# Weights turned into float32 in pieces of 768 columns, under a planner that books the SBUF port of GpSimd and VectorE

## The chip, the core and the metric

One core of a Trainium2 chip. The time is that of the device for one run of the program, in microseconds (us), here the median of three runs. Engines, as the profile names them: PE is TensorE's matmuls, PEld its weight loads, DVE is VectorE, ACT ScalarE, POOL GpSimd, SP the queue that issues the DMAs.

## The reference, cut to what matters

```python
def _attn_ref(x, weight_gen):               # x: 2 x 4096 x 192, weight_gen: 2 x 4096 x 8 x 7
    w = softmax(weight_gen, axis=-1)
    # token s: sum over the 7 taps of w[s, head, tap] * x[s - 6 + tap, head's 24 columns]
    out = np.einsum('bshk,bskhg->bshg', w, x_unf)

def _moe_ref(x, w_in, w_out):               # 8192 x 192, 192 x 2048, 2048 x 192
    h = x @ w_in
    g = h * np.cos(h)
    return g @ w_out

def _moe2_ref(x, w_in, w_out):
    h = x @ w_in
    g = np.maximum(0.01 * h, h)
    return g @ w_out

return _moe2_ref(_moe_ref(_attn_ref(x, weight_gen)))
```

The four weight matrices arrive as float64.

## The kernel before

**Tiling.** The 8192 tokens are cut into 16 blocks of 512. For each block the attention is a sum of seven products on VectorE (lines 385 to 414, tiles `pr` and `xa`; for blocks 0 and 1 the sum is made by PE, lines 461 to 476), which PE turns over so that columns lie on partitions. Then come the two layers, `m` = 0 and 1. A layer of one block is 16 chunks of 128 hidden columns. A chunk is ten matmuls of 512 columns: five make `h` (line 645, function `hidden`), five add its share to the block's output (`project_hi`, lines 694 to 696, and `project_lo`, lines 699 and 700). Every operand of a matmul is split in a rounded part `hi` and a remainder `lo`, which is why there are five.

**Between the two halves of a chunk.** In layer 0: ACT makes `g` from `h` (`turns`, line 657), DVE takes whole turns off (`angle`, 664), ACT takes the sine (669), DVE multiplies by `h` (`times`, 672), ACT rounds to `hi` (line 230, a helper), POOL subtracts to `lo` (line 235, a helper). In layer 1: ACT twice (681 and 230), then DVE for `lo`. `h` lies in PSUM, in one of three banks that chunks may hold; `g`, `hi` and `lo` lie in SBUF. So `angle` and `times` read PSUM, while the attention's `pr` and `xa` read and write SBUF alone.

**Weights.** A layer's weights come in four groups (four chunks each), so there are eight groups, and all eight are needed early, since a first block of layer 1 starts at chunk 32 of 512. A group comes in four pieces: `a` (128 x 512), `r` (128 x 256) of the first matrix, and `0` and `2` (128 x 384 each) of the second. Each piece is loaded as float64 words and then goes through ACT (`size`, line 564), POOL (`clamp`, 567), DVE (`shift`, 572), DVE (`merge`, 578), ACT (`low`, 585), POOL (`add`, 590); then `hi` parts are rounded (line 230 or 232) and POOL subtracts the `lo` parts (line 235: tiles `ilo`, `wlo`, `olo`, `or`).

**What sets the order.** `Plan` holds every operation with a due time, a cost for each engine that may do it, and its dependencies. `emit` walks through a plan's time and writes each engine's instructions down in that order. On the chip each engine then takes its own list strictly in order and waits by semaphores; nothing of the plan's times is left there. A cost that is written as a tuple is that of a DVE operation on SBUF alone; before, such a cost is multiplied by `SHARED` = 1.55 while POOL is busy.

Of the kernel before, what the change touches and what calls it, by code (L numbers as in the profile page):

```python
# [11 lines left out]
I32 = mybir.dt.int32  # L12
# [26 lines left out]
class Op:  # L39
    def __init__(self, due, cost, fn, deps, bufs):  # L40
        self.due, self.cost, self.fn, self.bufs = due, cost, fn, bufs
        self.deps, self.next, self.ready, self.end = len(deps), [], 0.0, None
        for d in deps:
            d.next.append(self)


class Plan:


    HOP = 0.08  # L50
    SLACK = 0.5
    NEAR = 0.12
# [3 lines left out]
    SHARED = 1.55  # L56
# [27 lines left out]
    def emit(self):  # L84
        free = dict.fromkeys(("PE", "ACT", "DVE", "POOL", "SP"), 0.0)
        wire = 0.0
# [5 lines left out]
        def start_of(o, e):  # L92
            t = max(o.ready + (self.SLACK if e == "PE" else 0.0), free[e], wire - 2.0 if e == "SP" else 0.0)
            if e == "SP" and o.due > self.at + self.AHEAD:
                return None
            for b in o.bufs:
# [8 lines left out]
            return t  # L105

        left = len(self.ops)
        while left:
            best = None
            for e in free:  # L110
# [10 lines left out]
                if at:  # L121
                    t0 = min(a[0] for a in at)
                    t, _, o = min((a for a in at if a[0] <= t0 + self.NEAR), key=lambda a: a[1])
                    if best is None or t < best[0]:
                        best = t, e, o
# [3 lines left out]
            if isinstance(cost, tuple):  # L129
                cost = cost[0] * (self.SHARED if free["POOL"] > t else 1.0)  # L130
# [25 lines left out]
            for n in o.next:  # L156
                n.ready = max(n.ready, o.end + self.HOP)
# [10 lines left out]
def conv_attention_moe_moe(ctx, tc, x, weight_gen, w_in1, w_out1, w_in2, w_out2, out):  # L168
# [27 lines left out]
    SUMMED = {0, 1}  # L196
    PACE = {0: 0.4, 1: 0.6}
# [81 lines left out]
    def softmax(s0, s1, due):  # L279
# [20 lines left out]
        op(due - 5, {"DVE": 0.2 + 0.95 * part}, lambda e: nc.vector.tensor_reduce(  # L300
            out=M(), in_=W(), axis=AX.X, op=ALU.max), [k], [k], bufs)
        op(due - 4, {"DVE": (0.2 + 0.85 * part,), "POOL": 0.3 + 1.6 * part}, lambda e: wide(e, ALU.subtract), [k], [k], bufs)
        op(due - 3, {"ACT": 0.2 + 0.8 * part + (2.6 if s0 else 0)}, lambda e: nc.scalar.activation(
            out=W(), in_=W(), func=AF.Exp), [k], [k], bufs)
        op(due - 2, {"DVE": 0.2 + 0.95 * part}, lambda e: nc.vector.tensor_reduce(
            out=M(), in_=W(), axis=AX.X, op=ALU.add), [k], [k], bufs)
        op(due - 2, {"DVE": 0.25}, lambda e: nc.vector.tensor_scalar(
            out=M(), in0=M(), scalar1=1e-9, scalar2=None, op0=ALU.add), [k], [k], bufs)
        op(due - 1, {"DVE": 0.25 + 0.7 * part}, lambda e: nc.vector.reciprocal(out=M(), in_=M()), [k], [k], bufs)
        op(due - 1, {"DVE": (0.2 + 0.85 * part,)}, lambda e: wide(e, ALU.mult), [k], [k], bufs)  # L310
# [40 lines left out]
    def attention(b, begins):  # L351
# [10 lines left out]
        for q0, q1, e0 in parts:  # L362
# [11 lines left out]
            for i, k in enumerate(reversed(range(K))):  # L374
# [4 lines left out]
                cost = (0.09 + 0.195 * n,) if e0 == "DVE" else 0.3 + 0.6 * n  # L379
# [42 lines left out]
                if e0 == "DVE":  # L422
                    main, rest = (cost[0] * 0.75,), (0.36 if n == Q else 1.1,)
# [19 lines left out]
    def attention_summed(b, begins):  # L443
# [7 lines left out]
        for i, k in enumerate(reversed(range(K))):  # L451
# [27 lines left out]
            op(due, {"DVE": (0.87,)}, product, reads, [("pr", b, k)], [xt, smw, pr])  # L479
            op(due + 0.5, {"PE": 0.9}, total, [("pr", b, k), "ident"] + ([("tm", b)] if i else []), [("tm", b)], [pr, tm])  # L480
            if i:
# [5 lines left out]
                op(due + 0.4, {"DVE": (0.36,)}, total_rest, keys, [("xbr", b, 0)], bufs)  # L487
# [17 lines left out]
    def place(m, b, due, key, src, v):  # L505
# [15 lines left out]
    def weights(m, g):  # L521
# [9 lines left out]
        def load(i, raw):  # L531
            if i == "a":
                nc.sync.dma_start(out=raw().rearrange("p c w -> p (c w)"), in_=wi[:P, c2])
            else:
                c = slice((g * GF + i) * P, (g * GF + i + 2) * P)
                nc.sync.dma_start(
                    out=raw().rearrange("p f d w -> p f (d w)"), in_=wo[c, :].rearrange("(f p) d -> p f d", p=P)
                )

        def load_rest(raw, j):  # L540
            c = slice(c2.start + 2 * j * half, c2.start + 2 * (j + 1) * half)
            nc.sync.dma_start(out=raw()[j * R : (j + 1) * R].rearrange("p c w -> p (c w)"), in_=wi[P:, c])

        for i in ("a", "r", 0, 2):
            shape = {"a": [GF * P], "r": [half]}.get(i, [2, D])
            w = math.prod(shape) / 512
            due = need[m, g * GF + (i or 0 if i in (0, 2) else 0)] + {"a": -0.6, "r": -3.0}.get(i, 1.8)
            raw = temp([P] + shape + [2], "raw", RAW, f"w{n}{i}", I32)
            t = temp([P] + shape, "wa", WA, f"wt{n}{i}", I32)
            v = temp([P] + shape, "wn", WN, f"wn{n}{i}", I32)  # L550
            k = n, i
            if i == "r":
                for j in range(2):
                    op(due - 6, {"SP": 0.4}, lambda e, raw=raw, j=j: load_rest(raw, j), (), [("raw", k, j)], [raw])
                kr = [("raw", k, 0), ("raw", k, 1)]
            else:
                op(due - 6, {"SP": 3.2 * w}, lambda e, i=i, raw=raw: load(i, raw), (), [("raw", k)], [raw])
                kr = [("raw", k)]

            def high(raw=raw):  # L560
                return raw()[..., 1]

            def size(e, t=t, high=high):
                nc.scalar.activation(out=t().bitcast(F32), in_=high().bitcast(F32), func=AF.Abs)

            def clamp(e, t=t):
                eng[e].tensor_scalar(
                    out=t().bitcast(F32), in0=t().bitcast(F32), scalar1=MOST, scalar2=LEAST, op0=ALU.min, op1=ALU.max
                )

            def shift(e, t=t):
                nc.vector.tensor_scalar(
# [229 lines left out]
```

## Time and profile before

| | us |
|---|---|
| three runs | 1287.0, 1287.84, 1288.92 |
| median | 1287.84 |
| the profiled execution | 1289.18 |
| its span, first to last instruction | 1287.2 |
| PE busy | 1233.0 (96%) |
| DVE busy | 933.4 (73%) |
| ACT busy | 883.4 (69%) |
| POOL busy | 489.0 (38%) |

The busy time of PE is made up of 5120 matmuls of 512 columns, the same number in any version of this kernel, and some transposes and sums with 128 columns. What can be gained or lost is time in which PE waits or runs at the lower clock, and that lies where other engines deliver too late. So the profile is read by stages of the span.

### The profile page before, as it was taken

How to read it: one execution, taken by the hardware profiler on the slowest of the kernel's cores; microseconds unless marked ns; L12 is line 12 of the kernel's file. 1: busy time of each engine (PE TensorE's matmuls, PEld its weight loads, DVE VectorE, ACT ScalarE, POOL GpSimd, SP SyncE). 2: the span in 40 equal slices, each digit the busy share in tenths (PEclk: the TensorE clock that was granted, in tenths of full speed). 3: DMA queues.
4: the chain of work that ended last, by engine and by line, in shares of the span. 5: the costliest groups of instructions: out<-in, count | busy, mean ns of one | idle time of the engine just before them, and what ended most of it. 6: DMA issues, size and time to landing. Idle time of an engine off the chain costs nothing.

```text
span 1287.2 us, 15419 instructions
## 1 busy us (share of the span) xinstructions
PE 1233.0 (96%) x5416; PEld 995.6 (77%) x5416; DVE 933.4 (73%) x1343; ACT 883.4 (69%) x1642; POOL 489.0 (38%) x398
## 2 busy tenths in 40 slices
PE   5798799999999999999999999999999999999998
PEld 4576587777778878787788878788787877888886
DVE  7998998889875776849795595866869586554333
ACT  4688776787776766767676666667676676776654
POOL 5898872566332322323323232322323232232000
PEclk8999899999999999999999999999999999999999
DMA  5231420100001000010100101010010100000000
GB/s 162 79 127 52 143 72 13 58 32 1 1 1 44 1 15 29 1 58 1 43 1 2 43 1 44 1 51 1 1 44 1 44 1 13 1 1 13 1 13 25
DMA packets 15037, 39.50 MB, mean 31 GB/s; under 512 B 1781, under 2 KB 8307, under 8 KB 14961
## 3 DMA queue, kind: packets, MB, share of 16 engines
q1 hardware_dynamic: 14960, 38.53, 9.1%
q8 instruction: 42, 0.69, 0.2%
q14 instruction: 35, 0.28, 0.1%
HBM read 30.13 MB, written 6.29 MB: 28 GB/s over the span
## 4 chain that ended last, share of the span: by engine, by line
PE 58%; DVE 28%; ACT 7%; issue 4%; POOL 1%; DMA 1%; SPq 0%; ACTq 0%; DVEq 0%; POOLq 0%
PE h L645 29%; DVE pr L392 5%; DVE g L672 4%; DVE g L664 4%; PE acc1r L696 3%; PE acc1m L700 3%; PE acc1m L694 3%; PE acc1m L695 3%; PE acc1r L699 3%; PE acc0m L694 3%; DVE xa L399 3%; PE acc0r L696 3%; PE acc0m L695 3%; DVE lo L235 3%; PE acc0r L699 2%
## 5 line engine op out<-in xcount | busy, mean ns | idle before, releaser
L235 POOL TENSOR_TENSOR lo<-g,hi 128x512 fp32r<-128x512 f32 x256 | 358.6, 1402 | 622.1 <-ACT hi L230 552.9
L235 DVE TENSOR_TENSOR lo<-h,hi 128x512 fp32r<-128x512 f32 x256 | 175.5, 687 | 167.5 <-ACT hi L230 165.0
L669 ACT ACTIVATE g<-g 128x512 f32<-128x512 f32 x256 | 161.5, 631 | 146.5 <-DVE g L664 145.9
L672 DVE TENSOR_TENSOR g<-h,g 128x512 f32<-128x512 f32 x256 | 175.1, 687 | 82.9 <-ACT g L669 81.5
L664 DVE SCALAR_TENSOR_TENSOR g<-g,h 128x512 f32<-128x512 int32 x256 | 173.8, 681 | 56.6 <-ACT g L657 55.0
L681 ACT ACTIVATE h<-h 128x512 f32<-128x512 f32 x256 | 149.0, 582 | 86.2 <-PE h L645 85.6
L657 ACT ACTIVATE g<-h 128x512 int32<-128x512 f32 x256 | 151.2, 591 | 61.0 <-PE h L645 60.0
L230 ACT ACTIVATE hi<-g 128x512 fp32r<-128x512 f32 x242 | 152.0, 630 | 36.2 <-DVE g L672 34.2
L230 ACT ACTIVATE hi<-h 128x512 fp32r<-128x512 f32 x256 | 151.4, 592 | 6.5 <-PE acc1r L696 0.2
L694 PE MATMUL acc0m<-hi,ohi 128*128 128x512 f32 x256 | 105.0, 410 | 16.5 <-ACT hi L230 14.9
L645 PE MATMUL h<-x0hi,ihi 128*128 128x512 f32 x256 | 102.4, 400 | 4.1 <-DVE g L672 2.7
L699 PE MATMUL acc0r<-lo,or 128*128 128x512 f32 x256 | 102.4, 400 | 3.0 <-POOL lo L235 3.0
L699 PE MATMUL acc1r<-lo,or 128*128 128x512 f32 x256 | 100.6, 393 | 3.7 <-DVE lo L235 3.6
L694 PE MATMUL acc1m<-hi,ohi 128*128 128x512 f32 x256 | 102.5, 400 | 0.1
L645 PE MATMUL h<-x1hi,ihi 128*128 128x512 f32 x256 | 101.8, 398 | 0.8 <-DVE g L672 0.8
L645 PE MATMUL h<-x0rh,r 128*128 128x512 f32 x256 | 101.0, 395 | 1.1 <-ACT x0rh L230 1.1
L695 PE MATMUL acc1m<-hi,olo 128*128 128x512 f32 x256 | 100.1, 391 | 1.8 <-POOL olo L235 1.8
L645 PE MATMUL h<-x1hi,ilo 128*128 128x512 f32 x256 | 100.5, 393 | 1.4 <-POOL ilo L235 1.4
L645 PE MATMUL h<-x0lo,ihi 128*128 128x512 f32 x256 | 100.6, 393 | 0.7 <-DVE x0lo L235 0.7
L645 PE MATMUL h<-x0hi,ilo 128*128 128x512 f32 x256 | 100.8, 394 | 0.0
L645 PE MATMUL h<-x0rl,r 128*128 128x512 f32 x256 | 100.6, 393 | 0.0
L645 PE MATMUL h<-x1rl,r 128*128 128x512 f32 x256 | 100.3, 392 | 0.1
(227 smaller groups left out, 2529.4 us busy)
## 6 DMA issues: line engine op xcount, KB each, us to landing
xt<-in_x SPq DMA_DIRECT2D x14, 960.0 KB, 4.8
w<-in_moe_w_out SPq DMA_DIRECT2D x16, 384.0 KB, 3.2
out<-osb SPq DMA_DIRECT2D x16, 384.0 KB, 2.6
smw<-in_weight_gen SPq DMA_DIRECT2D x3, 448.0 KB, 5.5
r<-whi SPq DMA_DIRECT2D x16, 64.0 KB, 3.1
r<-wlo SPq DMA_DIRECT2D x16, 64.0 KB, 2.1
xt<-in_x SPq DMA_DIRECT2D x1, 768.0 KB, 10.2
xt<-in_x SPq DMA_DIRECT2D x2, 283.5 KB
```

The costliest lines, as they stand in the source:

```text
L230: nc.scalar.activation(out=out, in_=in_, func=AF.Copy)
L235: eng[e].tensor_tensor(out=out, in0=a, in1=b.bitcast(F32), op=ALU.subtract)
L645: nc.tensor.matmul(h(), w[:, c], v(), start=i == 0, stop=i == len(terms) - 1)
L657: nc.scalar.activation(out=k, in_=h(), func=AF.Copy, scale=0.5 / math.pi, bias=0.25)
L664: nc.vector.scalar_tensor_tensor(out=g(), in0=g().bitcast(I32), scalar=-2 * math.pi, in1=h(), op0=ALU.mult, op1=ALU.add)
L669: nc.scalar.activation(out=g(), in_=g(), func=AF.Sin, bias=math.pi / 2)
L672: nc.vector.tensor_tensor(out=g(), in0=h(), in1=g(), op=ALU.mult)
L681: op(pos + 0.6, {"ACT": 0.58}, lambda e: nc.scalar.activation(out=h(), in_=h(), func=AF.Prelu, alpha=0.01), [kh], [kg], [h])
L694: nc.tensor.matmul(am(), ohi[:, f % GF, :], ghi(), start=first, stop=False)
L695: nc.tensor.matmul(am(), olo[:, f % GF, :], ghi(), start=False, stop=False)
L696: nc.tensor.matmul(ar(), orr[:, f % GF, :], ghi(), start=first, stop=False)
L699: nc.tensor.matmul(ar(), orr[:, f % GF, :], glo(), start=False, stop=last)
```

## The change

The notes at the planner's constants, and the operations, change in three ways.

**The pieces.** A group of weights now comes in two pieces, `in` (the old `a` and `r` side by side) and `out` (the old `0` and `2`), 128 x 768 each. The loads stay as they were, but `size`, `clamp`, `shift`, `merge`, `low` and `add` run over 768 columns at once; only for the first group, `PARTED`, are they kept apart (512 and 256, 384 and 384). The roundings and remainders of `out` also run over all four chunks of a group at once. The tiles `raw`, `wa` and `wn` have two buffers each instead of three.

**The early chunks.** For odd chunk numbers below `EARLY` = 34 in layer 0, `times` writes back into the PSUM bank of `h`, `hi` is rounded from there, and `lo` is made by DVE instead of POOL. There are 16 such chunks. Their bank is held until `lo` is made.

**The planner.** A variable `port` is set to the end of every POOL operation and of every DVE operation with a tuple as its cost, and such an operation is not planned to start before it; the factor 1.55 goes. Many costs are written anew, the time from PE to another engine gets `DRAIN` = 0.17 on top, and among operations that could start within `NEAR` = 0.6 the earliest due time wins, with a penalty for idle time. `turns`, `hi` of layer 1, `size` and `low` may now also go to DVE.

The core of the diff:

```diff
-    HOP = 0.08
+    HOP = 0.06
     SLACK = 0.5
-    NEAR = 0.12
+    NEAR = 0.6
+    IDLE = 20.0
 ...
-    SHARED = 1.55
+    DRAIN = 0.17
+    YIELD = 0.01
 ...
+            if e == "POOL" or isinstance(o.cost[e], tuple):
+                t = max(t, port)
 ...
             if isinstance(cost, tuple):
-                cost = cost[0] * (self.SHARED if free["POOL"] > t else 1.0)
+                cost = cost[0]
+                port = t + cost
+            elif e == "POOL":
+                port = t + cost
 ...
-        for i in ("a", "r", 0, 2):
-            shape = {"a": [GF * P], "r": [half]}.get(i, [2, D])
+        U = 3 * half
+        for i in ("in", "out"):
 ...
+            if (m, g) not in PARTED:
+                parts, loaded = [(0, U)], [loaded[0] + loaded[1]]
 ...
-            op(pos + 0.5, {"ACT": 0.58}, turns, [kh], [kg], [h, g])
+            op(pos + 0.5, {"ACT": 0.58, "DVE": 0.67}, turns, [kh], [kg], [h, g])
 ...
-            op(pos + 2.0, {"POOL": 1.42}, lambda e: minus(e, glo(), g(), ghi()), [kg, khi], [klo], [g, ghi, glo])
+            if bank_low:
+                op(pos + 1.4, {"DVE": 0.67}, times, [kg], [kh], [h, g])
+                op(pos + 1.7, {"ACT": 0.585, "DVE": 0.67}, lambda e: copy(e, ghi(), h()), [kh], [khi], [h, ghi])
+                op(pos + 2.0, {"DVE": 0.67}, lambda e: minus(e, glo(), h(), ghi()), [kh, khi], [klo], [h, ghi, glo])
 ...
-            op(pos + 1.0, {"ACT": 0.58}, lambda e: copy(e, ghi(), h()), [kg], [khi], [h, ghi])
+            op(pos + 1.0, {"ACT": 0.58, "DVE": 0.67}, lambda e: copy(e, ghi(), h()), [kg], [khi], [h, ghi])
```

What it moves, by the order of the built programs. PE's 5198 rows are the same work in another order. First POOL, the list around the remainders of the second group (`01`), before:

```order
L567 TENSOR_SCALAR wt01r_304<-wt01r_304 128x256
L567 TENSOR_SCALAR wt01a_298<-wt01a_298 128x512
L590 TENSOR_TENSOR wn01r_316<-wt01r_304,wn01r_316 128x256
L235 TENSOR_TENSOR wlo01_344<-wn01r_316,whi01_338 128x256
L590 TENSOR_TENSOR wn01a_313<-wt01a_298,wn01a_313 128x512
L567 TENSOR_SCALAR wt010_352<-wt010_352 128x384
L235 TENSOR_TENSOR lo_0_376<-g_0_289,hi_0_362 128x512
L235 TENSOR_TENSOR ilo01_85<-wn01a_313,ihi01_84 128x512
L235 TENSOR_TENSOR olo00_82<-wn002_278,ohi00_81 128x256
L235 TENSOR_TENSOR or00_83<-wn002_278,or00_83 128x2x64
L235 TENSOR_TENSOR lo_1_410<-g_1_327,hi_1_399 128x512
```

and POOL at the same place now:

```order
L607 TENSOR_SCALAR wt01in_278<-wt01in_278 128x768
L264 TENSOR_TENSOR olo00_82<-wn00out_208,ohi00_81 128x256 x2
L264 TENSOR_TENSOR or00_83<-wn00out_208,or00_83 128x2x64 x2
L631 TENSOR_TENSOR wn01in_287<-wt01in_278,wn01in_287 128x768
L264 TENSOR_TENSOR wlo01_360<-wn01in_287,whi01_324 128x256
L607 TENSOR_SCALAR wt01out_326<-wt01out_326 128x768
L264 TENSOR_TENSOR lo_0_375<-g_0_296,hi_0_339 128x512
L264 TENSOR_TENSOR ilo01_85<-wn01in_287,ihi01_84 128x512
```

Two clamps and two additions have become one each, and the remainder of chunk 1 (`lo_1`) is gone from POOL: it stands in DVE's list. Next DVE in the steady part, around chunk 160 (layer 0, block 6), where the attention of block 7 (`xa7`, `pr7`) is worked off between chunks, before:

```order
L399 TENSOR_TENSOR xa7_4010<-xa7_4010,pr7_4_4062 128x768
L672 TENSOR_TENSOR g_158_4142<-h0_6_2_4120,g_158_4142 128x512
L392 TENSOR_TENSOR pr7_3_4170<-xt7_3892,smw24_3096 128x768
L399 TENSOR_TENSOR xa7_4010<-xa7_4010,pr7_3_4170 128x768
L235 TENSOR_TENSOR lo_159_4191<-h1_3_12_4146,hi_159_4176 128x512
L664 SCALAR_TENSOR_TENSOR g_160_4189<-g_160_4189,h0_6_3_4180 128x512
```

and DVE at the same place now:

```order
L428 TENSOR_TENSOR xa7_3864<-xa7_3864,pr7_5_3735 128x768
L729 TENSOR_TENSOR g_158_3987<-h0_6_2_3961,g_158_3987 128x512
L264 TENSOR_TENSOR lo_159_4013<-h1_3_12_3979,hi_159_4006 128x512
L421 TENSOR_TENSOR pr7_4_4023<-xt7_3726,smw24_2921 128x768
L719 SCALAR_TENSOR_TENSOR g_160_4030<-g_160_4030,h0_6_3_4017 128x512
L428 TENSOR_TENSOR xa7_3864<-xa7_3864,pr7_4_4023 128x768
L729 TENSOR_TENSOR g_160_4030<-h0_6_3_4017,g_160_4030 128x512
```

One attention operation stands ahead of the angle of chunk 160 where there were two in a row. On PE, 22 matmuls lay between the end of `h` of chunk 160 and the first use of its `hi`, and 30 before the first use of its `lo`; now 25 and 28, and `lo` comes right behind the three matmuls with `hi`.

## Rows read from the trace of the kernel before

**Rows 1.** Busy time by stage of the span, with counts; first line names the columns.

```profile
core 0: us, PE busy (x) PEld busy (x) DVE busy (x) ACT busy (x) POOL busy (x), PEclk, DMA share, GB/s
0.00:24.00 24.00, 10.62 (x59) 9.78 (x60) 17.74 (x25) 6.51 (x13) 11.40 (x18) 1.00 0.61 166
24.00:70.00 46.00, 36.34 (x151) 27.91 (x150) 43.55 (x60) 33.47 (x69) 38.08 (x38) 0.85 0.32 98
70.00:120.00 50.00, 48.40 (x207) 37.47 (x206) 43.98 (x60) 43.36 (x89) 45.40 (x45) 1.00 0.28 88
120.00:162.00 42.00, 32.79 (x117) 24.00 (x116) 39.33 (x52) 32.43 (x67) 36.24 (x38) 0.84 0.41 124
162.00:282.00 120.00, 117.26 (x525) 95.20 (x524) 107.94 (x152) 88.92 (x166) 62.45 (x46) 1.00 0.14 47
282.00:1122.00 840.00, 827.13 (x3650) 669.48 (x3649) 609.31 (x885) 578.33 (x1062) 272.19 (x198) 1.00 0.05 17
1122.00:1283.00 161.00, 160.02 (x715) 131.61 (x713) 71.60 (x113) 99.52 (x180) 23.28 (x18) 1.00 0.02 8
...
138.00:146.00 8.00, 4.26 (x8) 2.51 (x9) 7.84 (x11) 7.11 (x17) 7.90 (x9) 0.51 0.39 101
```

**Rows 2.** The same view for the 128-column matmuls (those with `ident`) alone.

```profile
24.00:70.00 46.00, 9.58 (x58) 8.87 (x58) 0.00 (x0) 0.85 0.32 98
...
282.00:1122.00 840.00, 20.61 (x126) 16.36 (x126) 0.00 (x0) 1.00 0.05 17
```

**Rows 3.** Waits of PE: us in total, times, longest; stages 24–70, 120–162, 282–1122.

```profile
PE acc0m L694 <- ACT hi L230: 4.0, 2, 2.2
...
PE acc1r L699 <- DVE lo L235: 3.3, 1, 3.3
...
PE acc0m L694 <- ACT hi L230: 9.7, 21, 0.6
```

**Rows 4.** DVE's groups by shape, 0 to 162 us: busy us, mean ns, idle before.

```profile
L461 DVE TENSOR_TENSOR pr<-xt,smw 128x768 f32<-128x768 f32 x14 | 16.7, 1204 | 2.0 <-DMA xt<-in_x 1.8
L578 DVE SCALAR_TENSOR_TENSOR wt<-w,wt 128x384 int32<-128x384 int32 x13 | 12.7, 979 | 0.2
L572 DVE TENSOR_SCALAR wt<-wt 128x384 int32<-128x384 int32 x13 | 12.2, 935 | 0.9 <-POOL wt L567 0.9
```

**Rows 5.** Single lines' durations: ns shortest/median/longest, first and last start.

```profile
L461 DVE TENSOR_TENSOR pr<-xt,smw x14: 942/1177/1750, 7.4 to 51.0; 128x768 f32<-128x768 f32 x14
L572 DVE TENSOR_SCALAR wt<-wt x16: 342/885/1474, 23.4 to 183.9; 128x384 int32<-128x384 int32 x16
L578 DVE SCALAR_TENSOR_TENSOR wt<-w,wt x16: 543/778/1649, 23.8 to 184.3; 128x384 int32<-128x384 int32 x16
L578 DVE SCALAR_TENSOR_TENSOR wt12a<-w12a,wt12a x1: 676/676/676, 155.0 to 155.0; 128x512 int32<-128x512 int32 x1
L590 POOL TENSOR_TENSOR wn<-wt,wn x16: 999/1010/1734, 24.5 to 184.9; 128x384 int32<-128x384 int32 x16
L590 POOL TENSOR_TENSOR wn11a<-wt11a,wn11a x1: 1276/1276/1276, 134.6 to 134.6; 128x512 int32<-128x512 int32 x1
```

**Rows 6.** The page's costliest groups: remainders made by POOL and by DVE.

```profile
L235 POOL TENSOR_TENSOR lo<-g,hi 128x512 fp32r<-128x512 f32 x256 | 358.6, 1402 | 622.1 <-ACT hi L230 552.9
L235 DVE TENSOR_TENSOR lo<-h,hi 128x512 fp32r<-128x512 f32 x256 | 175.5, 687 | 167.5 <-ACT hi L230 165.0
```

**Rows 7.** Timeline of the steady part: start us, us, what.

```profile
522.24 1.45 DVE L392 TENSOR_TENSOR pr<-xt,smw 128x768 f32<-128x768 f32 x1
...
523.18 1.67 POOL L235 TENSOR_TENSOR lo<-g,hi 128x512 fp32r<-128x512 f32 x1 [0.30 <-ACT hi L230]
...
523.73 1.93 DVE L399 TENSOR_TENSOR xa<-xa,pr 128x768 f32<-128x768 f32 x1
...
526.18 0.67 DVE L664 SCALAR_TENSOR_TENSOR g<-g,h 128x512 f32<-128x512 int32 x1
...
529.21 0.50 PE L694 MATMUL acc0m<-hi,ohi 128*128 128x512 f32 x1 [0.61 <-ACT hi L230]
```

More of the change, by code (lines that the diff above doesn't have):

```diff
@@ L156, in emit @@
             for n in o.next:
-                n.ready = max(n.ready, o.end + self.HOP)
+                if e == "PE":
+                    n.own = max(n.own, o.end + self.HOP + self.DRAIN)
+                else:
+                    n.ready = max(n.ready, o.end + self.HOP)
                 n.deps -= 1
@@ L196, in conv_attention_moe_moe @@
     SUMMED = {0, 1}
+    EARLY = 34
+    PARTED = {(0, 0)}
     PACE = {0: 0.4, 1: 0.6}
@@ L613, in weights @@
-            hi = temp([P, half], "whi", 1, f"whi{n}", F32R)
-            lo = temp([P, half], "wlo", 1, f"wlo{n}", F32R)
-            op(due - 1.6, {"ACT": 0.42, "DVE": (0.4,)}, lambda e, hi=hi, t=t: copy(e, hi(), t().bitcast(F32)), [kt], [(k, "whi")], [t, hi])
-            op(due - 0.9, {"POOL": 0.85}, lambda e, hi=hi, lo=lo, v=v: minus(e, lo(), v().bitcast(F32), hi()),
-               [kv, (k, "whi")], [(k, "wlo")], [v, hi, lo])
-            for j in range(2):
-                c = slice(j * half, (j + 1) * half)
-                r = slice(j * R, (j + 1) * R)
-                for name, src, rows in (("hi", hi, slice(0, R)), ("lo", lo, slice(R, P))):
-                    op(due, {"SP": 0.4}, lambda e, src=src, rows=rows, c=c, r=r: nc.sync.dma_start(
-                        out=ir[rows, c].bitcast(F32), in_=src()[r].bitcast(F32)), [(k, f"w{name}")], [(k, name, j)], [src])
@@ new lines, in weights @@
+            for h, l, part, w2, (kc, j), pn, late in cut:
+                op(due - 1.6 + late, {"ACT": 0.18 + 0.46 * w2, "DVE": (0.15 + 0.275 * w2,)},
+                   lambda e, h=h, t=t, part=part: copy(e, h, part(t().bitcast(F32))), [kts[pn]], [(kc, "hi", j)], [t])
+                op(due - 0.9 + late, {"POOL": 0.18 + 1.1 * w2},
+                   lambda e, h=h, l=l, v=v, part=part: minus(e, l, part(v().bitcast(F32)), h),
+                   [kvs[pn], (kc, "hi", j)], [(kc, "lo", j)], [v])
@@ L628, in conv_attention_moe_moe, with low_in_bank @@
+            if i == "out" and len(parts) == 1:
+                for p in ("hi", "lo"):
+                    for j in range(2):
+                        plan.writers[(n, 2), p, j] = plan.writers[(n, 0), p, j]
     acc_of = {}
     sums_of = {}
+    def low_in_bank(pos):
+        return pos < EARLY and pos % 2 == 1
     def chunk(pos, st, m, b, f):
```

214 lines of the change are left out of this document (126 added, 88 removed).

## The prediction

> **What bounds the kernel now.** The stages come first, since PE is busy 96% of the span and an average over it hides where the rest lies. At its full pace a matmul of 512 columns follows the one before after 0.227 us, one of 128 columns after 0.111 us (differences of starts in the trace); the stage from 1122 to 1283 us, 715 matmuls in 161.00 us with PE busy for 160.02, shows that pace held [rows 1]. Counting a stage's matmuls at that pace gives what it lost. From 24 to 70 us: 93 of 512 columns and 58 of 128 [rows 1, 2], 21.1 + 6.4 = 27.5 us of work in 46, so 18.5 lost. From 70 to 120: 207 x 0.227 = 47.0, 3.0 lost. From 120 to 162: 117 x 0.227 = 26.6, 15.4 lost. From 162 to 282: PE is idle for 2.7. From 282 to 1122: 3524 x 0.227 + 126 x 0.111 = 813.9 of 840, 26.1 lost. Before 24 us there is only the softmax and the first block's attention.
>
> Who is late in the two bad stages? DVE is busy for 43.55 of 46 us in the one and for 39.33 of 42 in the other [rows 1]; PE waits for `hi`, `lo` and weights, all of them behind DVE or POOL [rows 3]. The granted clock there is 0.85 and 0.84, a mixture of the two levels 2.4 and 1.2 GHz. It fell after PE had waited: from 138 to 146 us, where its wait of 3.3 us lies, it is 0.51 and eight matmuls run [rows 1, 3]. So a wait costs twice.
>
> Then the question is what DVE does in that time. Its operations on SBUF alone take far longer than they need: `shift` of 384 columns has a mean of 935 ns against a shortest of 342, `merge` 979 against 543, the products of the first blocks 1204 against 942 [rows 4, 5]. These three alone are (935 - 342) x 13 + (979 - 543) x 13 + (1204 - 942) x 14 = 7.7 + 5.7 + 3.7 = 17.1 us above their shortest; the same sum over all 195 DVE instructions up to 162 us is 41 us. Operations of DVE that read PSUM show no such thing: 687 ns is both mean and rule for `lo` [rows 6]. The steady part shows the cause one by one: `xa` starts at 523.73, POOL has been at a `lo` since 523.18 and ends at 524.85, and `xa` takes 1.93 us, about the 1.0 that POOL still needs and its own 0.95 [rows 7]. So a DVE operation on SBUF waits until POOL's present instruction ends, and the other way about. In the first 162 us this is 41 of DVE's 144.6 busy us [rows 1].
>
> The Trainium skill, SBUF — State Buffer, section Who interferes with whom, states it as an exclusive lock of a port pair that is held for the whole instruction. The trace agrees (1.93 us above). The rule speaks against one half of this change: an instruction over 768 columns holds the lock longer than one over 384. That is the first rival below.
>
> **The change, part by part, up to 162 us.** I compare the two orders at the start of chunk 8 of layer 1, block 0, which the kernel before begins at about 159 us. Instruction counts are from the orders, durations are the shortest of each shape.
> - Pieces. DVE has 16 shifts and 16 merges there instead of 27 and 27. For 768 columns I extend the lines through 384 and 512: merge 543 to 676 ns, so 0.94; shift, by the same kind of line from 342, 0.55; add 999 to 1276, so 1.8 [rows 5]; the clamps are small. DVE: 24.3 us of shifts and merges become 21.5, so -2.8. POOL: clamps, adds and the weights' remainders go from 56.4 to 52.8, so -3.6. The elements stay; only fixed parts go.
> - Early chunks. 16 remainders leave POOL, undisturbed about 1.28 us each (their mean is 1.402 [rows 6]), -20.5 us; DVE takes them at 0.687, +11.0.
> - Other work that now stands on DVE before that point: five `turns` and five roundings from PSUM, ten at 0.68 = +6.8; two more remainders of layer 1, +1.4; against that four roundings of weights (-1.4) and one softmax product that POOL takes (-1.1, and +1.8 there).
> - Sum: DVE +13.9 us of work, POOL -22.3.
>
> So DVE, the engine that was late, gets more to do. What it may get back is its 41 us of waiting. There were 101 DVE operations on SBUF against 129 POOL instructions by then, 0.41 us of waiting for each; now 74 against 82. DVE before: 144.6 busy = 103.6 of work and 41 of waiting, and 17.4 idle [rows 1]. Now: 103.6 + 13.9 + 17.4 = 134.9 plus a waiting W that no trace shows. Below: W = 0, if the order keeps the two apart all the time. Above: the same 0.41 for each of 74 operations, times the longer POOL instruction (92 us in 82 against 114 in 129, 1.12 against 0.88 us, a factor of 1.27), so W = 38. A plan that books the port should beat chance, but its times are not enforced on the chip, and an error of a few tenths of a us brings a wait back. I take the middle, W = 18, so the point comes at 153 us and not 162: 9 us. By then PE has been given 430 matmuls of 512 columns where it had 408, 22 x 0.227 = 5.0 us more of its work is done, and from there on PE sets the pace. **Early part: -14 us**, between about -26 (W near 6; below that PE's own waits for data at the start remain) and +6 (W = 38).
>
> **The steady part, 282 to 1122 us.** PE waits 21 times for ACT's `hi`, 9.7 us in all [rows 3]; with the restart of PE and smaller gaps this is most of the 26.1. The same three gaps come back in eight periods of 76 us, one for each block. The largest of them, in the rows: `pr` 1.45 and `xa` 1.93 stand in a row, so the angle behind them starts at 526.18 only, and PE waits at 529.21 [rows 7]. The new order has one attention operation there and 25 matmuls (5.67 us) instead of 22 (4.99) up to `hi`. Against it, `lo` is now needed after 28 matmuls, 6.36 us, not 30. POOL needs about 1.3 us for it, so `hi` must be there some 5.0 us after `h` either way. The gain hangs on DVE's delay, then, not on PE's order: one contended operation (0.95 to 1.4) ahead of an angle instead of two (3.4). I take it that about half of the 26.1 goes: **-14 us**, between 0 and -21.
>
> The end (1122 to 1287 us) has no loss to give back [rows 1]. SP issues 80 rows instead of 88, the same bytes; loads wait for two buffers and not three, which costs nothing as long as a piece of weights, some 6 us of work, is not late, and the bad stages hold DVE, not DMA.
>
> **Sum.** Against the profiled execution of 1289.18 us (span 1287.2, and 2.0 around it): -28 gives 1261.2; the median of the runs lies 1.3 below the profiled one, so 1287.84 - 28 = **1260 us**.
>
> **Rivals.**
> - *The longer instructions block.* Nothing in the lists is enforced, and if meetings at the port are as frequent as by chance, W is about 30 (0.41 x 74, a little more for the longer instructions and a little less as POOL is busy for less of the time). The point comes at 165 us, with the 5 us of PE's work -2 in all; the steady part gives 10. 1276 us. By the Trainium skill's rule above this is what an order that knows nothing of the lock would do.
> - *Only the early part gains.* In the steady part POOL's `lo` and the attention meet as now: 1287.84 - 14 = 1274 us.
> - *Nearly all goes.* W near 6 and 5 us of loss in the steady part: 1287.84 - 26 - 20 = 1242 us.
> - *Slower: DVE's extra work lands in the chunks.* From 282 us on the new order gives DVE 15 `turns` and 40 roundings of layer 1 from PSUM, 55 x 0.68 = 37 us, against ten short roundings less. Each stands in a chain from `h` to `hi`. If 31 of them delay PE by their 0.68, the steady part loses 21 us on top of the 26 that stay: 1287.84 - 14 + 21 = 1295 us. It ends slower once more than 21 of the 55 do (14 / 0.68). For it: `lo` close behind `hi` leaves little room. Against it: DVE is busy for only 609 of 840 us there [rows 1].
> - That the change does not do what it says is ruled out by the orders shown.
>
> **Chances.** Forecast 0.52; blocking 0.15; early part alone 0.12; nearly all 0.09; slower 0.09; no effect to speak of 0.03. A difference of 0.2%, 2.6 us, is about what a measurement of this kernel can tell from none. Faster by more than that: 0.88; within: 0.03; slower: 0.09. The range of 8 in 10 reaches from the best case to W = 38 with a small gain in the steady part, 1242 to 1283 us.
>
> **What would show it.** Right: DVE's shifts and merges near their shortest (for 768 columns 0.55 and 0.94), the matmul count of 120 to 162 us well over 117 and the clock there near 1.00, and fewer than ten waits of PE for `hi` between 282 and 1122. Wrong: DVE's waiting up to 162 us still at 30 or more; PE waiting for `lo` where it waited for `hi`; waits of `h` for a PSUM bank, since the odd early chunks hold theirs through rounding and remainder, some 1.4 us longer.

## The result: 1248.9 us, and the profile after

| | before | after |
|---|---|---|
| median of the runs, us | 1287.5 | 1248.9 |
| lowest and highest, us | 1287.0, 1288.9 | 1247.4, 1249.8 |
| the profiled execution, us | 1289.18 | 1249.18 |
| its span, us | 1287.2 | 1247.4 |

The changed kernel takes 0.970 of the time before (95% interval 0.968 to 0.971), 38.6 us less. Forecast were 28 us less, 1260 us, in a range of 1242 to 1283.

The view that led the prediction is that of the stages. For the changed kernel (the columns are those of [rows 1]):

```profile
24.00:70.00 46.00, 37.02 (x159) 27.32 (x160) 40.32 (x61) 32.33 (x60) 31.68 (x25) 0.87 0.31 88
70.00:120.00 50.00, 49.16 (x210) 39.59 (x209) 43.96 (x70) 44.21 (x80) 34.70 (x29) 0.98 0.39 117
120.00:162.00 42.00, 39.23 (x157) 31.06 (x157) 37.58 (x52) 34.33 (x59) 29.65 (x22) 0.92 0.36 107
162.00:282.00 120.00, 118.57 (x534) 97.29 (x534) 104.93 (x156) 86.89 (x162) 54.23 (x39) 1.00 0.11 38
282.00:1122.00 840.00, 839.83 (x3765) 694.08 (x3764) 606.93 (x940) 573.79 (x1054) 283.42 (x201) 1.00 0.05 17
...
138.00:146.00 8.00, 8.00 (x37) 6.64 (x36) 7.28 (x12) 7.87 (x15) 5.96 (x5) 1.00 0.30 98
```

Against [rows 1]: from 120 to 162 us PE runs 157 matmuls where it ran 117, and the stretch from 138 to 146 us, which had eight of them at a granted clock of 0.51, has 37 at 1.00. From 282 to 1122 us PE has no idle time to speak of, 839.83 of 840 us busy.

Counted as in the prediction (the length of a stage less its matmuls at 0.227 and 0.111 us), and beside it the waiting in DVE's and POOL's instructions (what each lasts above the shortest of its own shape, summed):

| stage, us | PE lost, before | after | DVE waiting, before | after | POOL waiting, before | after |
|---|---|---|---|---|---|---|
| 0 to 24 | 17.3 | 17.3 | 4.1 | 4.5 | 2.4 | 1.3 |
| 24 to 70 | 18.7 | 16.9 | 13.1 | 5.7 | 7.4 | 5.6 |
| 70 to 120 | 3.5 | 2.8 | 9.5 | 3.3 | 3.7 | 1.5 |
| 120 to 162 | 15.9 | 6.6 | 14.2 | 6.9 | 6.4 | 4.4 |
| 162 to 282 | 4.8 | 2.5 | 14.4 | 7.8 | 17.1 | 6.6 |
| 282 to 1122 | 26.3 | 0.9 | 66.0 | 32.1 | 21.3 | 27.2 |

The first five rows give 14.1 us back (11.8 of them before 162 us), the last 25.4. One place says the same without the bounds of stages: the start of `h` of layer 0, block 4, behind the same amount of PE's work in both orders, moves from 281.8 to 267.8 us, by 14.0.

The waits of PE, answering to [rows 3]: the three largest from 24 to 162 us, and then the one wait between 282 and 1122 us (columns: us in total, times, longest).

```profile
PE tm L495 <- DVE pr L490: 3.3, 3, 1.9
PE h L700 <- DVE x0rl L261: 2.4, 2, 1.9
PE acc0m L756 <- ACT hi L259: 2.0, 3, 1.5
...
PE acc0r L761 <- POOL lo L264: 0.2, 1, 0.2
```

Of the 21 waits for ACT's `hi` in the steady part none is left. There the attention's operations on DVE, by shape, have these times (busy us, mean ns), first before, then after:

```profile
L392 DVE TENSOR_TENSOR pr<-xt,smw 128x768 f32<-128x768 f32 x65 | 76.3, 1174 | 0.3
L399 DVE TENSOR_TENSOR xa<-xa,pr 128x768 f32<-128x768 f32 x55 | 64.9, 1181 | 0.4
```

```profile
L421 DVE TENSOR_TENSOR pr<-xt,smw 128x768 f32<-128x768 f32 x66 | 63.8, 967 | 0.0
L428 DVE TENSOR_TENSOR xa<-xa,pr 128x768 f32<-128x768 f32 x55 | 52.8, 960 | 0.4
```

They run near their shortest, 0.95 us. One stretch in which this can be followed is in the timeline of the changed kernel (start us, us, what), the counterpart of [rows 7]:

```profile
506.37 0.95 DVE L421 TENSOR_TENSOR pr<-xt,smw 128x768 f32<-128x768 f32 x1
...
508.62 0.95 DVE L428 TENSOR_TENSOR xa<-xa,pr 128x768 f32<-128x768 f32 x1
...
508.85 1.87 POOL L264 TENSOR_TENSOR lo<-g,hi 128x512 fp32r<-128x512 f32 x1 [3.21 <-ACT hi L259]
...
510.90 0.95 DVE L421 TENSOR_TENSOR pr<-xt,smw 128x768 f32<-128x768 f32 x1
```

POOL's last remainder ends at 505.64 and `pr` begins at 506.37; the next remainder ends at 510.72 and the next `pr` begins at 510.90. In between they do meet once: `lo` is issued while `xa` runs and lasts 1.87 us instead of 1.28. But here POOL does the waiting, whose `lo` PE doesn't yet need, and DVE does not, behind which an angle is queued. The table says the same of the whole part: DVE's waiting halves, POOL's grows from 21.3 to 27.2 us.

### The profile page after: what moved, and what is told of

Its sections match the earlier page's. It is cut to its first block, busy times and chain, and to the rows that moved or that the text cites. A ratio compares the mean times of both kernels' runs of the same rounds, so it can differ in the third digit from the quotient of the medians.

```text
span 1247.4 us, 15239 instructions
## 1 busy us (share of the span) xinstructions
PE 1216.0 (97%) x5416; PEld 998.9 (80%) x5416; DVE 903.2 (72%) x1381; ACT 848.4 (68%) x1549; POOL 456.2 (37%) x341
## 4 chain that ended last, share of the span: by engine, by line
PE 89%; DVE 6%; ACT 2%; DMA 1%; issue 1%; POOL 0%; SPq 0%; DVEq 0%; ACTq 0%; POOLq 0%
PE h L700 44%; PE acc1m L762 5%; PE acc1r L761 5%; PE acc1m L756 5%; PE acc1r L758 5%; PE acc1m L757 5%; PE acc0r L761 4%; PE acc0m L762 4%; PE acc0m L756 4%; PE acc0r L758 4%; PE acc0m L757 4%; DVE g L719 1%; DVE pr L490 1%; DMA xt<-in_x 1%; DVE g L729 1%
## 5 line engine op out<-in xcount | busy, mean ns | idle before, releaser
L264 POOL TENSOR_TENSOR lo<-g,hi 128x512 fp32r<-128x512 f32 x240 | 339.2, 1415 | 598.3 <-ACT hi L259 481.5
L264 DVE TENSOR_TENSOR lo<-h,hi 128x512 fp32r<-128x512 f32 x272 | 186.4, 687 | 93.3 <-ACT hi L259 90.9
L712 ACT ACTIVATE g<-h 128x512 int32<-128x512 f32 x233 | 138.2, 595 | 135.7 <-PE h L700 135.2
L729 DVE TENSOR_TENSOR g<-h,g 128x512 f32<-128x512 f32 x240 | 164.4, 686 | 37.1 <-ACT g L724 31.5
L259 ACT ACTIVATE hi<-g 128x512 fp32r<-128x512 f32 x236 | 148.2, 629 | 48.2 <-DVE g L729 46.7
L259 ACT ACTIVATE hi<-h 128x512 fp32r<-128x512 f32 x226 | 134.3, 594 | 9.5 <-DVE h L729 1.5
L756 PE MATMUL acc0m<-hi,ohi 128*128 128x512 f32 x256 | 101.9, 398 | 3.7 <-ACT hi L259 2.0
L762 PE MATMUL acc0m<-lo,ohi 128*128 128x512 f32 x256 | 100.2, 392 | 0.0
L700 PE MATMUL h<-x1rh,r 128*128 128x512 f32 x256 | 100.2, 391 | 0.0
L700 PE MATMUL h<-x1lo,ihi 128*128 128x512 f32 x256 | 100.2, 391 | 0.0
```

The lines of the kernel that those rows point to most:

```text
L259: nc.scalar.activation(out=out, in_=in_, func=AF.Copy)
L264: eng[e].tensor_tensor(out=out, in0=a, in1=b.bitcast(F32), op=ALU.subtract)
L700: nc.tensor.matmul(h(), w[:, c], v(), start=i == 0, stop=i == len(terms) - 1)
L712: nc.scalar.activation(out=k, in_=h(), func=AF.Copy, scale=0.5 / math.pi, bias=0.25)
L729: nc.vector.tensor_tensor(out=h() if bank_low else g(), in0=h(), in1=g(), op=ALU.mult)
L756: nc.tensor.matmul(am(), ohi[:, f % GF, :], ghi(), start=first, stop=False)
```

## The experiments

All ratios are to the kernel before, on the same chip, with 95% intervals. Its own median was 1287.5 to 1288.4 us there, so times of different runs compare to within about a us.

### The pieces alone undone

```diff
-    PARTED = {(0, 0)}
+    PARTED = {(m, g) for m in range(2) for g in range(4)}
```

> The changed kernel (1248.9 us) with one part undone: every group's weights go through size, clamp, shift, merge, low and add in the old pieces of 512, 256, 384 and 384 columns. Theory of the prediction (only fixed parts are saved, 2.8 us of VectorE and 3.6 of GpSimd up to 162 us): 1250 to 1253 us, all of it before 162 us. Rival (longer instructions hold the port longer, so short pieces are better): 1245 to 1248 us, with less waiting of VectorE than the 20 us above its shortest durations that the changed kernel shows up to 162 us. The steady part (282 to 1122 us) loses nothing in either.

1252.5 us, 0.973 (0.971 to 0.974): the change in piece width, which gives the change its name, is worth 3.6 of the 38.6 us. DVE's waiting up to 162 us is the same with the old widths (20.7 us) as with the new ones (20.4), so the longer instructions do not block more. That leaves the fixed parts of the instructions, as the expectation has it, but that was not tried by itself.

### The early chunks undone

```diff
-    EARLY = 34
+    EARLY = 0
```

> The changed kernel with EARLY = 0: the 16 odd early chunks get their remainders from GpSimd again, and free their PSUM bank after the product. Theory (GpSimd's instructions are what VectorE waits for, so taking 20 us of them away pays): VectorE's excess up to 162 us goes from 20 back to 30 or more, time 1255 to 1262 us. Rival (VectorE is the bound and 11 us more work on it only costs, or the bank held longer costs): 1240 to 1247 us.

1258.0 us, 0.977 (0.975 to 0.978). The time is the one that the first view expected, but DVE's waiting up to 162 us is 25.3 us and not 30 or more. 9.2 us are lost, in the stages from 24 to 162 us (19.4, 5.1 and 10.9 us of PE lost instead of 16.9, 2.8 and 6.6); the steady part keeps its 0.9. POOL is busier for it from 70 to 120 us: 46.01 us, with 199 matmuls on PE, against 34.70 and 210.

```profile
70.00:120.00 50.00, 46.77 (x199) 36.52 (x198) 38.53 (x55) 38.87 (x69) 46.01 (x37) 1.00 0.31 91
```

### Half as many early chunks

```diff
-    EARLY = 34
+    EARLY = 17
```

> The changed kernel with EARLY = 17 instead of 34: eight early chunks and not sixteen. Theory 1 (each early chunk relieves POOL by about the same): half of the 9.2 us that all sixteen give, 1253 to 1254. Theory 2 (the relief counts while POOL also prepares weights and PE waits, mostly past 70 us): nearly all is lost, 1256 to 1258. Theory 3 (it counts at the start): 1249 to 1250.

1250.0 us, 0.970 (0.969 to 0.972). The first eight give nearly all of the 9.2 us, 8.0 of them, as the third theory had it.

### Both undone

```diff
-    EARLY = 34
-    PARTED = {(0, 0)}
+    EARLY = 0
+    PARTED = {(m, g) for m in range(2) for g in range(4)}
```

> The changed kernel with the old piece widths for all eight groups (PARTED holds every group) and without early chunks (EARLY = 0); booking, DRAIN and the pick rule stay. Theory 1 (the two parts give back different time: 3.6 us and 9.2 us lost when each alone is undone): 1248.9 + 3.6 + 9.2 = 1261 to 1263, with DVE's waiting up to 162 us about 25 and the steady part still under 1.5 us of loss. Theory 2 (both relieve the same thing, POOL in the first 162 us, and so support each other): more than 1266, since without either one POOL's work comes back in full. Theory 3 (they overlap): about 1258, no worse than without early chunks alone.

1263.7 us, 0.980 (0.979 to 0.982). 14.8 us are lost, 12.8 would be the sum of the two: they add up within 2 us, and the steady part keeps its 0.9. The third theory fell; the time lies 0.7 us above the first one's range and below the second one's 1266.

### The booking undone

The lines that keep an operation from starting before `port` are taken out, and the factor 1.55 is put back.

```diff
-            if e == "POOL" or isinstance(o.cost[e], tuple):
-                t = max(t, port)
...
-                cost = cost[0]
-                port = t + cost
+                cost = cost[0] * (1.55 if free["POOL"] > t else 1.0)
```

> The changed kernel whose planner does not book the port: no operation waits for it in the plan, and VectorE's operations on SBUF cost 1.55 times as much while GpSimd is busy, as before. All else is as changed. Theory 1 (booking the port took the loss out of the steady part): PE loses 12 to 25 us between 282 and 1122 us again, time 1262 to 1280 us. Theory 2 (it is the later use of hi by PE, from the time allowed to a matmul's end, or the rule by which operations are picked): the steady part loses under 5 us, time 1250 to 1256 us.

1268.1 us, 0.985 (0.983 to 0.986): 19.2 us are lost, more than by any other part that was undone alone. About half of it, 10.0 us, is lost up to 282 us, and 9.0 in the steady part. Here is the steady part by its stage row:

```profile
282.00:1122.00 840.00, 838.17 (x3722) 683.70 (x3723) 649.91 (x960) 559.79 (x1019) 287.48 (x201) 1.00 0.05 17
```

and by the shapes of `pr` and `xa`:

```profile
L418 DVE TENSOR_TENSOR pr<-xt,smw 128x768 f32<-128x768 f32 x65 | 82.1, 1263 | 0.0
L425 DVE TENSOR_TENSOR xa<-xa,pr 128x768 f32<-128x768 f32 x54 | 56.3, 1042 | 0.3
```

DVE waits more there than in the kernel before, 82.6 us against 66.0, and yet PE loses only 9.9 us and not 26.3. The time is in the first theory's range, but the steady part's loss is in neither's (12 to 25, or under 5). So some other part of the change lets DVE wait longer without making PE late.

### Booking, DRAIN and the pick rule undone

```diff
-    NEAR = 0.6
-    IDLE = 20.0
+    NEAR = 0.12
+    IDLE = 0.0
...
-    DRAIN = 0.17
+    DRAIN = 0.0
```

on top of the edit before.

> The changed kernel without the planner's three new means together: no booking of the port (the factor 1.55 instead), DRAIN = 0, the old pick rule. New costs, the pieces, the early chunks and the choices of engine stay. If the three means carry the steady part, PE loses some 20 to 26 us between 282 and 1122 us as in the kernel before, and 1275 to 1285 us is the time. If the new costs carry it, under 12 us are lost there, as without the booking alone, and the time is 1264 to 1272 us.

1278.0 us, 0.992 (0.990 to 0.994). Now the steady part loses 22.7 us, with DVE's waiting at 93.4; its stage row:

```profile
282.00:1122.00 840.00, 826.96 (x3667) 670.99 (x3666) 641.03 (x918) 568.49 (x1039) 278.78 (x197) 1.00 0.05 17
```

and PE's largest wait there:

```profile
PE acc0m L753 <- ACT hi L256: 11.1, 13, 1.2
```

That is the picture of the kernel before [rows 1, 3]. Without a booking, `DRAIN` and the pick rule together hold back 12.8 us there (22.7 - 9.9).

### DRAIN alone undone, the pick rule alone undone

```diff
-    DRAIN = 0.17
+    DRAIN = 0.0
```

> The changed kernel with DRAIN = 0: the plan again believes that other engines can go on 0.06 us after a matmul's end. In the steady part the median number of matmuls between the end of h and the first use of hi in layer 0 falls from 25 to 20. Theory A (the later use of hi carries part of the steady part's gain): PE loses 4 to 10 us between 282 and 1122 us, time 1253 to 1260 us. Theory B (the port's booking alone carries it): under 2 us lost there, time 1247 to 1251 us.

```diff
-    NEAR = 0.6
-    IDLE = 20.0
+    NEAR = 0.12
+    IDLE = 0.0
```

> The changed kernel with the old rule for picking an operation (NEAR = 0.12, no penalty for idle time); the port is still booked. Theory A (the new rule lets an operation of a chunk that is ready 0.6 us later go ahead of the attention's, so chains from h to hi stay short): PE loses 4 to 10 us between 282 and 1122 us and some us more before 162; 1254 to 1262 us. Theory B: no more than 2 us anywhere, 1247 to 1251 us.

Without `DRAIN` 1250.8 us (0.971, 0.969 to 0.972), with the old pick rule 1250.4 us (0.971, 0.969 to 0.972): with the port booked, each alone is worth 1.5 to 2 us, about what can be told from nothing, and the steady part loses 0.4 and 1.0 us, as the second theory had it for both.

### No alternatives on DVE

`turns` and the `hi` of layer 1 may not go to DVE.

```diff
-            op(pos + 0.5, {"ACT": 0.58, "DVE": 0.67}, turns, [kh], [kg], [h, g])
+            op(pos + 0.5, {"ACT": 0.58}, turns, [kh], [kg], [h, g])
...
-            op(pos + 1.0, {"ACT": 0.58, "DVE": 0.67}, lambda e: copy(e, ghi(), h()), [kg], [khi], [h, ghi])
+            op(pos + 1.0, {"ACT": 0.58}, lambda e: copy(e, ghi(), h()), [kg], [khi], [h, ghi])
```

> The changed kernel in which turns and the rounding of layer 1 may not go to VectorE any more. The slower rival of the prediction (VectorE's extra work delays the chunks) would have it faster, below 1246 us. The forecast's view (VectorE has room in the steady part, and these moves relieve ACT's queue): 1248 to 1252 us, the steady part without loss either way.

1248.5 us, 0.969 (0.968 to 0.971), no difference from the changed kernel, though DVE's waiting in the steady part falls to 16.0 us. The slower rival's mechanism, 55 operations more on DVE, costs nothing there: neither with them nor without them does PE lose a us (0.9 and 0.7).

### The booking alone

The kernel before, with the lines of the booking put in and the factor 1.55 taken out.

```diff
+            if e == "POOL" or isinstance(o.cost[e], tuple):
+                t = max(t, port)
...
-                cost = cost[0] * (self.SHARED if free["POOL"] > t else 1.0)
+                cost = cost[0]
+                port = t + cost
+            elif e == "POOL":
+                port = t + cost
```

> The kernel before (1287.5 us) with the booking of the port alone put into its planner, in place of the factor 1.55; its costs, pick rule, pieces and early chunks as before. Theory 1: the steady part's loss of 26 us falls to under 10, time 1262 to 1272 us. Theory 2: the steady part still loses 20 us or more, time 1280 to 1290 us.

1290.5 us, 1.001 (1.0005 to 1.002). The expected 1262 to 1272 was missed. The steady part does what was expected (`pr` and `xa` at 957 and 969 ns, DVE's waiting 34.5 us, PE loses 7.2), but up to 282 us PE loses 20.6 us more than before: 80.8 against 60.2. Two of its stage rows:

```profile
70.00:120.00 50.00, 40.06 (x158) 30.20 (x157) 40.80 (x55) 39.07 (x76) 42.27 (x38) 0.92 0.31 91
282.00:1122.00 840.00, 837.29 (x3738) 687.69 (x3737) 584.04 (x909) 596.75 (x1088) 290.01 (x206) 1.00 0.05 17
```

`pr` and `xa` of the steady part, by shape:

```profile
L397 DVE TENSOR_TENSOR pr<-xt,smw 128x768 f32<-128x768 f32 x66 | 63.2, 957 | 0.3
L404 DVE TENSOR_TENSOR xa<-xa,pr 128x768 f32<-128x768 f32 x55 | 53.3, 969 | 0.2
```

PE's largest wait between 70 and 170 us:

```profile
PE acc0r L704 <- POOL lo L240: 18.2, 8, 6.0
```

PE waits for POOL's remainders, up to 6.0 us at a time. We read it so: POOL and DVE are both nearly full between 70 and 120 us ([rows 1]: 45.40 and 43.98 of 50), and a plan that lets only one of the two use SBUF puts POOL's work off. The wait is shown, this reason for it is not.

### What the early part needs beside the booking

Two runs close in on it from both sides. The first is the changed kernel with everything undone but the booking and the rewritten costs and weights' code (old piece widths, no early chunks, `DRAIN`, `NEAR` and `IDLE` as above).

```diff
-    EARLY = 34
-    PARTED = {(0, 0)}
+    EARLY = 0
+    PARTED = {(m, g) for m in range(2) for g in range(4)}
...
-    NEAR = 0.6
-    IDLE = 20.0
-    DRAIN = 0.17
+    NEAR = 0.12
+    IDLE = 0.0
+    DRAIN = 0.0
```

> As the run before, and DRAIN = 0, NEAR = 0.12, IDLE = 0 on top: of the planner's changes only the booking and the newly written costs stay, the pieces are the old ones and there are no early chunks. The kernel before with booking alone took 1290.5 and lost some 20 us more up to 162 us, since PE waited there for POOL's remainders. Theory 1 (it was the pick rule and DRAIN that keep the early part from this): 1280 or more, PE waiting over 10 us for lo between 70 and 170 us. Theory 2 (it was the costs written anew, with which the plan knows how long POOL's and DVE's operations really take): within 4 us of the run before, 1260 to 1267, PE waiting under 5 us for lo there.

1268.9 us, 0.985 (0.984 to 0.986): 5.2 us above the run with both parts undone, a little over the limit that the second theory had set, and far from the first one's 1280. PE's wait for `lo` between 70 and 170 us is 7.1 us, between what the two had set (under 5, over 10); it is 6.0 in the run before. The 5.2 us come from the steady part, which loses 7.0 us and not 0.9; up to 162 us the two runs lose the same (59.0 and 58.7).

The second is the kernel before with the booking and the new costs of DVE and POOL, of which three:

```diff
-            op(due - 3.4, {"DVE": (0.12 + 0.45 * w,)}, shift, [kt], [kt], [t])
+            op(due - 3.4, {"DVE": (0.14 + 0.275 * w,)}, shift, [kt], [kt], [t])
...
-            op(due - 2, {"POOL": 0.2 + 1.3 * w}, add, [kt, kv], [kv], [t, v])
+            op(due - 2, {"POOL": 0.2 + 1.06 * w}, add, [kt, kv], [kv], [t, v])
...
-            op(pos + 2.0, {"POOL": 1.42}, lambda e: minus(e, glo(), g(), ghi()), [kg, khi], [klo], [g, ghi, glo])
+            op(pos + 2.0, {"POOL": 1.28}, lambda e: minus(e, glo(), g(), ghi()), [kg, khi], [klo], [g, ghi, glo])
```

> The kernel before with the booking and with the newly written costs of POOL's and DVE's operations (about twenty numbers, for example POOL's remainder 1.28 instead of 1.42, shift 0.14 + 0.275 per 512 columns instead of 0.12 + 0.45); its pieces, buffers, HOP and pick rule stay as before, and there are no early chunks. With the booking alone it took 1290.5; the changed kernel with the same things undone took 1268.9. Theory 1 (the costs make that difference, since a booked port with too long times leaves it empty and POOL late): 1266 to 1274, PE waiting under 8 us for POOL's lo between 70 and 170 us, and the loss up to 162 us near 59 instead of 71. Theory 2 (it is the rest of the edit: buffers for two pieces of 768 columns, the order of the loads, HOP): 1284 or more, with the wait for lo still over 12 us.

1286.7 us, 0.999 (0.998 to 1.000). The new costs are worth 3.8 us, where the first theory expected 16 or more. PE's wait for `lo` falls from 18.2 to 6.8 us, but it now waits for weights (between 70 and 170 us):

```profile
PE h L650 <- POOL ilo L240: 7.2, 2, 5.5
PE acc0r L704 <- POOL lo L240: 6.8, 8, 1.7
```

Neither theory is right as it stands: the time fits the second, the wait doesn't. The 17.8 us from here to the 1268.9 (up to 282 us, PE loses 79.4 against 60.8) lie in what is left of the edit: `raw`, `wa` and `wn` with two buffers of 768 columns, other due times of the weights' operations, the operations that may now go to DVE, `HOP`, and the small rules of the planner. Which of these it is was not tried.

The runs form a ladder:

| kernel | us |
|---|---|
| before | 1287.5 |
| + booking | 1290.5 |
| + new costs | 1286.7 |
| + the rest of the weights' and the planner's code | 1268.9 |
| + DRAIN and the pick rule | 1263.7 |
| + pieces and early chunks (the changed kernel) | 1248.9 |

The order of the steps matters: the booking gives nothing as the first of them (2.1 us more than the kernel before on the same chip) and 19.2 us as the last.

## Why the prediction was right, and where it was not

**What bounds the kernel: right in the main.** DVE's waiting on SBUF was named as what makes PE late, and the booking, which is aimed at it, gives the most of the parts that were undone alone. But the sum of that waiting is not what PE loses by, as the steady part shows below.

**The early part: right in size, in part by luck.** -14 was forecast for the start of chunk 8 of layer 1, block 0; the stages up to 282 us give 14.1. That chunk was to start at 153 us and starts at 154.1, with 430 matmuls of 512 columns ahead of it, as the orders had it; W, the waiting left on DVE up to 162 us, was taken as 18 and is 20.4. But the prediction's 9 us count from 162 us, up to which its 144.6 us of busy time and its 27 shifts were counted, and not from the start of that chunk in the kernel before, 159.4 us. From there it is 5.3 us, and with the 5.0 of PE's work 10.3. The other 3.7 us come between that chunk and the start of block 4 of layer 0, of which the prediction said that PE sets the pace from there on. Two errors of 3.7 us cancel: a gain counted too high at that chunk, and a later gain put at nothing. The prices for 768 columns held too (durations in ns, shortest/median/longest, of one piece each; the lines are `shift`, `merge` and `add`):

```profile
L612 DVE TENSOR_SCALAR wt01out<-wt01out x1: 546/546/546, 43.0 to 43.0; 128x768 int32<-128x768 int32 x1
...
L618 DVE SCALAR_TENSOR_TENSOR wt01out<-w01out,wt01out x1: 944/944/944, 44.7 to 44.7; 128x768 int32<-128x768 int32 x1
...
L631 POOL TENSOR_TENSOR wn10out<-wt10out,wn10out x1: 1840/1840/1840, 121.3 to 121.3; 128x768 int32<-128x768 int32 x1
```

0.55, 0.94 and 1.8 were extended from 384 and 512 columns; 0.55, 0.94 and 1.84 these three took. Not right is the clock that was to show it: from 120 to 162 us it is 0.92, not near 1.00. PE still waits three times between 123 and 128 us, for `hi`, `lo` and `hi` (1.2, 1.0 and 0.5 us), and after that the granted clock from 126 to 134 us is 0.57 to 0.58. And the sum rested on DVE and W alone. The runs put the price of POOL's relief beside it: without early chunks W rises only to 25.3, yet 9.2 us are lost, and with the booking alone PE waits for POOL's `lo`, not for DVE. The prediction had POOL's -22 us in its list and gave them no price of their own.

**The steady part: mis-sized.** Forecast was that half of the 26.1 goes, -14; 25.4 went. This is nearly all of the miss (28 forecast, 38.6 measured). The failing step is the sentence that "about half" of the loss goes, one contended operation ahead of an angle instead of two; it lets the loss shrink in step with the waiting. The waiting did halve, 66.0 to 32.1, but the loss didn't follow it. It is a matter of a limit: PE loses only where `hi` or `lo` comes after the matmuls that lie ahead of its first use, and the rest of the waiting is free. The traces show it when each `hi` and `lo` is compared with PE's own list. In the table, one is counted as too late if it was ready less than 0.1 us before PE, at its full pace, had done the matmuls ahead of it, or later; each run has some 720 in the steady part. The last column is the time by which PE starts such matmuls, and those right behind them, later than at its pace.

| kernel | DVE waiting, us | PE lost, us | too late | lost at these, us |
|---|---|---|---|---|
| before | 66.0 | 26.3 | 41 | 22.6 |
| neither booking nor DRAIN and pick rule | 93.4 | 22.7 | 33 | 19.1 |
| DRAIN and pick rule, no booking | 82.6 | 9.9 | 22 | 7.8 |
| before + booking | 34.5 | 7.2 | 15 | 5.6 |
| booking, no DRAIN and pick rule | 30.1 | 7.0 | 34 | 5.8 |
| before + booking + new costs | 54.5 | 5.2 | 6 | 2.5 |
| booking, no pick rule | 33.8 | 1.0 | 6 | 0.7 |
| changed kernel | 32.1 | 0.9 | 1 | 0.4 |
| booking, no DRAIN | 24.9 | 0.4 | 1 | 0.1 |

Most of what PE loses, where it loses over 5 us, is lost at operands that come too late (last column), except in the run with 54.5 us of waiting, where it is about half. The sum of the waiting doesn't set it: with 54.5 us PE loses 5.2, with 30.1 it loses 7.0. Two things bring the loss down, and each covers much of what the other does: the booking, and `DRAIN` or the pick rule. Each alone leaves 5 to 10 us, both leave 0.9. (The run with the booking and without `DRAIN` and the pick rule also has the old pieces and no early chunks; the run without these two parts alone loses 0.9 there, so they don't matter here.)

**"The gain hangs on DVE's delay, then, not on PE's order": right about PE's order, too simple about the delay.** The prediction compared the matmuls that lie ahead of `hi` and of `lo` at a single chunk and held that the limit stays at 5.0 us either way. Their number is indeed not what gains: the median between the end of `h` and the first use of `hi` in layer 0 is 22 in the kernel before, 25 in the run that loses 22.7 us, and 20 in the run without `DRAIN`, which loses 0.4. What changes is the time from `h` to `hi`: one in ten takes over 6.0 us in the kernel before, and over 5.0 in the changed one, where none takes longer than the matmuls ahead of it at their pace (54 of 180 do before). But this delay isn't the sum of DVE's waiting, as the table shows, and "one attention operation instead of two" does not hold beyond the place that was shown: of 196 attention operations in DVE's list 20 stood right ahead of another before, and 19 do now. Each has become shorter, 1.17 to 0.97 us. At which chunks `DRAIN` and the pick rule shorten the way from `h` to `hi` was not followed further.

**The rivals.** The blocking rival is out: W is 20.4 and not 30, and the old widths give the same 20.7. The Trainium skill, SBUF — State Buffer, section Who interferes with whom, says that the lock is held for the whole instruction. The trace agrees: a `shift` of 768 columns that starts at 93.36 us, behind a remainder that ends at 94.59, lasts 1.65 us instead of 0.55. But a plan that knows of it has less waiting, 32.1 us in the steady part with the booking and 82.6 without it. That only the early part gains is out by the table above. The nearly-all rival, 1242 us, had the steady part right (5 us left; 0.9 are) and the early part too good (-26). The slower one is out by the run without alternatives on DVE.

## What to carry to other kernels

A loss that comes from waits need not be in proportion to them: count for each operand whether it comes later than the work that the waiting engine still has ahead of it. Here half of the waiting went and nearly all of the loss with it (66.0 to 32.1 us, 26.3 to 0.9). Where GpSimd and VectorE both work on SBUF, try to plan them as one resource, but look at the places where both are nearly full: up to 282 us the booking cost 20.6 us in the old kernel and gave 10.0 in the changed one, which had taken work from GpSimd there and whose planner differed in more than that. And undo parts of a change from both ends, since a part that gives nothing by itself (the booking: +2 us on the old kernel) can be the largest one in company (19 us).

## What of the hardware was not expected

A meeting at the port mostly costs no more than the rest of one instruction of the other engine. In the changed kernel DVE's longest wait is 1.15 us (1.13 in the one before), about one remainder of POOL, and all of POOL's waits but one are under 0.9 us, about one operation of DVE. Also where an engine has one operation right behind another, the other engine mostly gets in between: in the traces of these 14 kernels there are 777 meetings in which the next operation on SBUF starts within 0.25 us, and in 769 of them it got in. So it is in the kernel before, where `wlo` ends at 20.60, between two products that stand in one row here and last until 21.42:

```profile
18.54 2.88 DVE L461 TENSOR_TENSOR pr<-xt,smw 128x768 f32<-128x768 f32 x2
19.28 1.32 POOL L235 TENSOR_TENSOR wlo<-wn00r,whi 128x256 fp32r<-128x256 f32 x1
```

But in the other eight a row of operations keeps the other engine out to its end. In the changed kernel DVE has four on SBUF (timeline):

```profile
45.54 0.41 DVE L505 TENSOR_TENSOR xb<-xb,pr 128x256 f32<-128x256 f32 x1
...
45.76 3.95 POOL L631 TENSOR_TENSOR wn01out<-wt01out,wn01out 128x768 int32<-128x768 int32 x1 [5.14 <-DVE wt01out L618]
45.88 1.81 DVE L490 TENSOR_TENSOR pr<-xt,smw 128x768 f32<-128x768 f32 x2
...
47.62 0.41 DVE L505 TENSOR_TENSOR xb<-xb,pr 128x256 f32<-128x256 f32 x1
```

The addition lasts 3.95 us instead of 1.81: it ends at 49.71, so its own work began at about 47.9, when the row was over, although three of the four began after it. The same addition is kept out in the runs with the old pieces (3.65 us for 384 columns, whose shortest is 0.99), without `DRAIN` (3.95), without the pick rule (2.75, behind a row of two), without alternatives (4.02) and with half the early chunks (3.95). It happens in the other direction too. In the run with both pieces and early chunks undone, a `shift` of 512 columns lasts 2.59 us instead of 0.41, until POOL's row of two clamps and a softmax product is over:

```profile
117.75 0.98 POOL L607 TENSOR_SCALAR wt10out<-wt10out 128x384 f32<-128x384 f32 x2
...
118.16 2.59 DVE L612 TENSOR_SCALAR wt10in<-wt10in 128x512 int32<-128x512 int32 x1
118.69 1.77 POOL L325 TENSOR_TENSOR smw<-smw,smm 128x896 f32<-128x896 f32 x1
```

It lasts 2.59 us again in the run that also lacks `DRAIN` and the pick rule. What sets these eight apart was not found.
